# A two-layer block behind a Fourier transform: the first layer's split passes take 512 columns from two neighbouring chunks

## The chip, the cores and the metric

One Trainium2 chip; the program runs on one of its cores. The metric is the device time of one execution in microseconds (us); lower is better. Engines: PE (TensorE, matrix products), DVE (VectorE), ACT (ScalarE), POOL (GpSimd) and SP, which issues most DMAs.

## The reference

A batch of 8 sequences of 3008 rows and 256 columns goes through a two-dimensional Fourier transform, of which the real part is kept. Its 24,064 rows then go through two layers with a hard-swish between them:

```python
X = np.fft.fft(x, axis=1)
X = np.fft.fft(X, axis=2)
x = X.real.astype(np.float32).reshape(B * S, D)      # 24064 x 256
h = x @ w_in                                         # 256 -> 2048
g = h * np.clip(h + 3.0, 0.0, 6.0) / 6.0
return (g @ w_out).astype(np.float32)                # 2048 -> 256
```

## The kernel before

**Tiling.** The batch is taken as 4 pairs of sequences. A pair's transform along the rows has two stages (47 x 64 points): stage 1 multiplies folded inputs (POOL folds them) with a table and writes `z` to DRAM; stage 2 loads it back as `g`, multiplies it with a table `T`, and leaves `q`, 256 transformed rows at a time. The transform along the 256 columns is not done by itself: it is multiplied into `w_in` at the start (`W1`). Real input makes the result symmetric, so each `q` has an even and an odd part (block 0 and block 1), and one sum of products serves a row and its mirror image: even + odd and odd - even.

**Chunks and steps.** A pair has 12 chunks of 256 columns of `q` (the last: 194 for the first layer, 192 for the second). A chunk has 8 steps, each with two blocks of 128 of the 2048 features. So there are 4 x 12 x 8 = 384 steps. Steps 0 to 21 (`SPLIT` = 22) use plain f32 products for the first layer while the weights are prepared; from then on the first layer is split.

**The split first layer.** `split_q` and `split_w` (L612 to L617, L625 on) write `q` and `W1` as three parts each in a format that PE takes in one pass. A step's first layer is then 3 parts x 2 blocks x 2 feature blocks = 12 passes of 256 columns (`half_products`, L639): six even ones into the PSUM banks `u` and `v` (`even_half`), and, one step later, six odd ones into the same banks (`odd_half`). One row of the product is missing from the even part, the row part: `spread` broadcasts the row of `q` that it needs over all partitions by two DMAs (`qd`, `qn`), and `add_row` (L653) adds `qn` times the weights' column `WN` to `v` on DVE, 256 columns at a time, into `d`.

**Between the layers,** for the 512 columns (two feature blocks) of a step: ACT copies v to `y` (L669); DVE forms u + v (L670), ACT its relu (L708); DVE forms the other sign from the saved even part `s` (L679, L660), ACT its relu; then two gates on DVE (L711), min(t, 1) x h, write the activations `a`, the second one reversed for the mirrored rows.

**The second layer** is a Strassen-like scheme: POOL makes four sums `c` of the `a` (`combine`, L725), PE takes 7 products of f32 per step (`mlp2`, L758; each stands as two records) into 4 PSUM banks `acc` over the 8 steps. At a chunk's end ACT copies the banks to `e` (`copy_sums`, L775), POOL adds them up (`finish`, L725, L783), DVE transposes (L828) and SP stores.

**Order.** It is written out by hand, step by step. Step s runs the odd passes for step s + 2, the second layer of step s, the even passes for step s + 3 and `combine` for s + 1. The PSUM banks `a0`, `a1` (for u) and `y0`, `y1` (for v) alternate by step, and stage 1 (both banks of a turn) and stage 2 (one) borrow them. `beside` puts loads, spreads, stage 1 and stage 2 at fixed steps; `Feed` gives POOL the folding of the next pair where its estimated backlog allows it. Pools `ypool`, `gpool`, `qpool` and `zpool` have two buffers each, activations three (`apool`).

The order of a step's instructions, as far as it isn't plain from the above:

```python
odd_half(*chunk(s + 2))                  # PE odd passes; y, u + v, first relu
mlp2(*chunk(s), 0, 1)
stage1_parts(t); run(middle_fns, t)      # stage 1, stage 2
even_half(*chunk(s + 3), s + 3, ...)
add_row(*chunk(s + 3)); other_sign(*chunk(s + 2))
keep_even(*chunk(s + 3))
first_gate(*chunk(s + 2)); second_gate(*chunk(s + 2))
sums(); mlp2(*chunk(s), n, 7)            # combine, finish, store, split_q, folding; products
```

Of the kernel before, what the change touches and what calls it, by code (L numbers as in the profile page):

```python
# [49 lines left out]
WS = 2.0 ** 20  # L50
# [10 lines left out]
def kernel(  # L61
# [39 lines left out]
    ypool = ctx.enter_context(tc.tile_pool(name="ypool", bufs=2))  # L101
    zpool = ctx.enter_context(tc.tile_pool(name="zpool", bufs=2))
    gpool = ctx.enter_context(tc.tile_pool(name="gpool", bufs=2))
    tpool = ctx.enter_context(tc.tile_pool(name="tpool", bufs=1))
    qpool = ctx.enter_context(tc.tile_pool(name="qpool", bufs=2))
    spool = ctx.enter_context(tc.tile_pool(name="spool", bufs=2))
    apool = ctx.enter_context(tc.tile_pool(name="apool", bufs=3))
# [18 lines left out]

    ctx.enter_context(tc.manual_schedule())

    F1 = consts.tile([P, 5 * PB], F32, name="F1")
# [4 lines left out]
    W1 = consts.tile([P, 2, FF], F32, name="W1")  # L134
# [4 lines left out]
    class Pair:  # L139
        def __init__(self, p):  # L140
            self.p = p
            self.x, self.xr, self.y, self.z = {}, {}, {}, {}
            self.zd = {} if p == 0 else None
            self.zq = None
            self.g, self.q, self.qn = {}, {}, {}
# [6 lines left out]
    def x_tile(pool=xpool, tag="x"):  # L152
        return pool.tile([P, XC, D], F32, tag=tag, name="xt")
# [62 lines left out]
    def fold_half(hb, m, part, eng):  # L216
# [11 lines left out]
        y = ypool.tile([PX - 1, XC + 1, D], F32, tag="y", name="y")  # L228
# [46 lines left out]
    def bank(shape, name):  # L275
        if starting[0]:
            return ps_a.tile(shape, F32, tag="acc", name=name)
        if turn_of[0]:
            return ps_u.tile(shape, F32, tag=f"y{turn_of[0] % 2}", name=name)
        return lone_tile(shape, name)  # L280

    def other_bank(shape, name):
        if turn_of[0]:
            return ps_u.tile(shape, F32, tag=f"a{turn_of[0] % 2}", name=name)
# [4 lines left out]
    def stage1(pr, c):  # L289
# [17 lines left out]
        nc.scalar.copy(z[:, 0], ps[0][0:PB + PZ])  # L307
# [133 lines left out]
    def load_g(pr, gr):  # L441
        g = gpool.tile([P, 2 * KK, D + 1], F32, tag="g", name="g")
# [25 lines left out]

    def stage2_half(hb, gr, copy=nc.scalar.copy, ps=None, tab=None):

        vg, i = hb.b * NSG // 2 + gr // 2, gr % 2
        if i == 0:
            first.q[vg] = qpool.tile([P, 2, 2 * TB], F32, tag="q", name="q")
# [18 lines left out]
    def row_tile(pr, i):  # L492
        pr.qn[i] = qpool.tile([P, 2 * TB], F32, tag="qn", name="qn")

    def spread_half(hb, gr):
        vg, i = hb.b * NSG // 2 + gr // 2, gr % 2
        if i == 0:
            row_tile(first, vg)
        cs = slice(i * TB, (i + 1) * TB)
        qd = dpool.tile([1, 2 * TB], F32, tag="qd", name="qd")  # L500
        nc.sync.dma_start(out=qd[:, cs], in_=first.q[vg][P - 1:P, 1, cs])
        nc.sync.dma_start(out=first.qn[vg][:, cs], in_=qd[:, cs].to_broadcast([P, TB]))
        del hb.g[gr]

    def spread_by_pe(hb, ps, tab):
        row_tile(first, 0)
# [3 lines left out]
        nc.scalar.copy(first.qn[0][:, 0:TB], ps)  # L510
        del hb.g[0]

    def stage2(pr, gr, i, copy=nc.scalar.copy):

        if i == 0:
            pr.q[gr] = qpool.tile([P, 2, 2 * TB], F32, tag="q", name="q")
# [15 lines left out]
    def spread(pr, gr):  # L532
        row_tile(pr, gr)
        n = 2 * TB if gr < NG - 1 else 3 * P + 2 * NH
        qd = dpool.tile([1, 2 * TB], F32, tag="qd", name="qd")
        nc.sync.dma_start(out=qd[:, 0:n], in_=pr.q[gr][P - 1:P, 1, 0:n])
        nc.sync.dma_start(out=pr.qn[gr][:, 0:n], in_=qd[:, 0:n].to_broadcast([P, n]))
        del pr.g[gr]

    class Chunk:  # L540
# [3 lines left out]
        def __init__(self, pr, ck):  # L544
# [7 lines left out]
            self.a, self.c, self.acc, self.front, self.k = {}, {}, {}, {}, None  # L552
# [5 lines left out]
            self.blocks = [[(2 * b[j] + h, (k1[j], N1 - k1[j])[m]) for j in range(KC) for h in range(2)]  # L558
                           for m in range(2)]
# [7 lines left out]
    def mlp1_products(ch, fc, between=None):  # L567
# [3 lines left out]
        for blk, ps in ((0, u), (1, v)):  # L571
# [3 lines left out]
            for i in range(2):  # L575
                f = 2 * fc + i
                nc.tensor.matmul(ps[:, i, 0:nq], W1[r, blk, f * P:(f + 1) * P], q[r, blk, of:of + nq],  # L577
                                 start=True, stop=True)
        return u, v

    def activate(ch, fc, u, v, between=None):
        of, nq, qn = ch.ck % 2 * TB, ch.nq, ch.pr.qn[ch.ck // 2]
        s = spool.tile([P, 2, TB], F32, tag="s", name="s")
        for i in range(2):
            f = 2 * fc + i
            nc.vector.scalar_tensor_tensor(s[:, i, 0:nq], qn[:, of:of + nq], WN[:, f:f + 1], u[:, i, 0:nq],  # L586
# [3 lines left out]
        a = apool.tile([P, 2, 2, TB], F32, tag="a", name="a")  # L590
        t = spool.tile([P, 2, 2, TB], F32, tag="t", bufs=1, name="t")
        ch.a[fc] = a
# [11 lines left out]
    def split_q(ch):  # L604

        of, nq, q = ch.ck % 2 * TB, ch.nq, ch.pr.q[ch.ck // 2]
        ch.k = qpool.tile([P, 3, 2, TB], F32R, tag="k", bufs=2, name="k")
        high, low, rest = (ch.k[:, j, :, 0:nq] for j in range(3))
# [25 lines left out]
    def half_products(ch, fc, blk, u, v, order=(2, 0, 1)):  # L634
        nq = ch.nq
        for j in order:
            for i in range(2):
                fs = slice((2 * fc + i) * P, (2 * fc + i + 1) * P)
                nc.tensor.matmul((u, u, v)[j][:, i, 0:nq], KW[:, j, blk, fs], ch.k[:, j, blk, 0:nq],  # L639
                                 start=(blk == i == 0 and j != 1), stop=True, skip_group_check=True)  # L640

    def even_half(ch, fc, step, order):
        u = ps_u.tile([P, 2, TB], F32, tag=f"a{step % 2}", name="u")
        v = ps_u.tile([P, 2, TB], F32, tag=f"y{step % 2}", name="v")
        half_products(ch, fc, 0, u, v, order)
        ch.front[fc] = [u, v]

    def add_row(ch, fc):
        of, nq, qn, (u, v) = ch.ck % 2 * TB, ch.nq, ch.pr.qn[ch.ck // 2], ch.front[fc]
        d = spool.tile([P, 2, TB], F32, tag="d", bufs=1, name="d")  # L650
        for i in range(2):
            f = 2 * fc + i
# [892 lines left out]
```

## Time and profile before

| | before |
|---|---|
| median of 3 runs (lowest to highest) | 1831.02 us (1831.0 to 1833.35) |
| the profiled execution | 1830.63 us |
| its span in the profile | 1828.9 us |
| granted clock of PE, mean | 0.999 |
| busy share PE, DVE, POOL, ACT | 99%, 89%, 84%, 53% |
| busy PE weight loads | 89% |

A row of the timeline has the start in us, the duration in us, the engine, the line, the operation, the tiles as out<-in, the shape and how many were merged (x4); in brackets the idle time of the engine before it and what ended it. A merged row's duration runs from the first start to the last end, and PE's records overlap their neighbours: from start to start is what counts. A row of the groups has the count, the busy time in us, the mean ns of one, and the idle time before.

### The profile page before, as it was taken

The page shows a single profiled execution, that of the slowest core. Times are in us where ns is not written, and L with a number is a line of the kernel's source. Part 1 is how long each engine was busy: PE and PEld are TensorE (multiplying, and loading weights), DVE is VectorE, ACT ScalarE, POOL GpSimd, SP SyncE. Part 2 cuts the span into 40 slices and gives each one's busy share as a digit, 9 for nine tenths or more (in the row PEclk, how much of TensorE's full clock was granted, in tenths as well). Part 3 has the DMA queues.
Part 4 walks back from the last instruction along what each step waited for, and adds up shares of the span by engine and source line. Part 5 has one row for each costly group of instructions (what it writes and reads, how often), then busy time and mean ns, then how long its engine had stood idle before and what let it go on. Part 6 is the DMA issues. An engine that isn't in the chain of part 4 may idle for free.

```text
span 1828.9 us, 32501 instructions
## 1 busy us (share of the span) xinstructions
PE 1815.0 (99%) x10896; PEld 1619.8 (89%) x10896; DVE 1622.3 (89%) x3132; ACT 962.4 (53%) x1630; POOL 1529.7 (84%) x1694
## 2 busy tenths in 40 slices
PE   9999999999999999999999999999999999999998
PEld 6688888889998888899999888889999999999997
DVE  8978888888998888888998888888989989899898
ACT  6554555555555555554555555555555555555543
POOL 5687999998789999987778999998778778777885
PEclk9999999999999999999999999999999999999999
DMA  7433242321122313111122232310111111101001
GB/s 274 116 98 95 74 102 60 75 60 41 45 63 75 89 41 94 40 48 29 30 61 65 61 84 56 90 50 22 36 40 30 45 30 30 41 18 47 18 13 33
DMA packets 157629, 110.54 MB, mean 60 GB/s; under 512 B 121952, under 2 KB 136090, under 8 KB 157462
## 3 DMA queue, kind: packets, MB, share of 16 engines
q1 hardware_dynamic: 148710, 82.22, 18.0%
q0 software_dynamic: 7504, 25.65, 4.6%
q8 instruction: 87, 1.43, 0.3%
q10 hardware_dynamic: 1248, 0.59, 0.1%
q14 instruction: 80, 0.66, 0.1%
HBM read 71.93 MB, written 36.79 MB: 59 GB/s over the span
## 4 chain that ended last, share of the span: by engine, by line
PE 90%; DVE 5%; DMA 2%; issue 1%; ACT 1%; POOL 1%; SPq 0%; DVEq 0%; ACTq 0%; POOLq 0%
PE acc L758 58%; PE u L639 18%; PE v L639 9%; PE ps L526 2%; DVE a L711 1%; PE ps L296 1%; PE v L577 1%; DMA xt<-in_x_dram,IT 1%; PE u L577 1%; PE acc L735 1%; DVE d L653 1%; DVE s L660 0%; DVE s L586 0%; ACT t L708 0%; DVE u L593 0%
## 5 line engine op out<-in xcount | busy, mean ns | idle before, releaser
L758 PE MATMUL acc<-c,G 128*128 128x256 f32 (+1 forms) x3008 | 697.4, 375 | 0.0
L758 PEld LDWEIGHTS acc<-c,G 128*128 128x128 f32 x3008 | 559.9, 190 | 70.1 <-POOL c L725 2.4
L758 PE MATMUL acc<-a,G 128*128 128x256 f32 (+1 forms) x2256 | 599.8, 376 | 0.0
L725 POOL TENSOR_TENSOR c<-a 128x512 f32<-128x512 f32 (+1 forms) x375 | 471.7, 1258 | 129.9 <-DVE a L711 113.8
L639 PE MATMUL u<-k,KW 128*128 128x256 f32 (+1 forms) x2880 | 468.6, 285 | 0.9 <-DVE s L660 0.7
L708 ACT ACTIVATE t<-u,half 128x512 f32<-128x512 f32 (+1 forms) x384 | 260.6, 679 | 311.7 <-DVE u L670 255.9
L758 PEld LDWEIGHTS acc<-a,G 128*128 128x128 f32 x2256 | 373.0, 189 | 37.3 <-issue 17.5
L639 PE MATMUL v<-k,KW 128*128 128x256 f32 (+1 forms) x1440 | 403.0, 361 | 1.0 <-DVE a L711 1.0
L639 PEld LDWEIGHTS u<-k,KW 128*128 128x128 f32 x2880 | 393.5, 189 | 6.5 <-DVE s L660 1.4
L669 ACT COPY y<-v 128x512 f32<-128x512 f32 (+1 forms) x360 | 207.7, 577 | 319.8 <-PE v L639 319.8
L708 ACT ACTIVATE t<-v,half 128x512 f32<-128x512 f32 (+1 forms) x384 | 260.3, 678 | 201.1 <-DVE v L679 200.5
L670 DVE SCALAR_TENSOR_TENSOR u<-u,y 128x512 f32<-128x512 f32 (+1 forms) x360 | 247.1, 686 | 110.5 <-ACT y L669 96.5
L653 DVE SCALAR_TENSOR_TENSOR d<-qn,WN,v 128x256 f32<-128x256 f32 (+1 forms) x720 | 307.1, 468 | 9.9 <-PE v L639 9.6
L639 PEld LDWEIGHTS v<-k,KW 128*128 128x128 f32 x1440 | 265.1, 190 | 36.4 <-PE u L639 1.5
L725 POOL TENSOR_TENSOR c<-a,c 128x256 f32<-128x256 f32 (+1 forms) x375 | 269.5, 719 | 29.4
L725 POOL TENSOR_TENSOR c<-c,a 128x256 f32<-128x256 f32 (+1 forms) x375 | 269.2, 718 | 29.4
L679 DVE SCALAR_TENSOR_TENSOR v<-s,u 128x512 f32<-128x512 f32 (+1 forms) x360 | 246.4, 684 | 51.9 <-ACT t L708 51.3
L711 DVE SCALAR_TENSOR_TENSOR a<-t,u 128x512 f32<-128x512 f32 (+2 forms) x448 | 260.4, 593 | 3.2 <-ACT t L708 3.2
L711 DVE SCALAR_TENSOR_TENSOR a<-t,v 128x512 f32<-128x512 f32 (+1 forms) x480 | 263.1, 565 | 0.1
L660 DVE SCALAR_TENSOR_TENSOR s<-u,d 128x512 f32<-128x512 f32 (+1 forms) x360 | 242.6, 674 | 2.5
L725 POOL TENSOR_TENSOR e<-e 128x512 f32<-128x512 f32 (+2 forms) x184 | 182.8, 994 | 0.1
L775 ACT ACTIVATE e<-acc 128x512 f32<-128x512 f32 (+2 forms) x184 | 98.6, 538 | 4.7 <-PE acc L758 4.2
(140 smaller groups left out, 1090.4 us busy)
## 6 DMA issues: line engine op xcount, KB each, us to landing
out_dram<-o SPq DMA_DIRECT2D x744, 32.0 KB
T<-in_c_stage_dram SPq DMA_DIRECT2D x26, 512.0 KB
g<-zd SPq DMA_DIRECT2D x42, 256.0 KB
zd<-z SPq DMA_DIRECT2D x48, 192.0 KB
xt<-in_x_dram SPq DMA_DIRECT2D x21, 256.0 KB
qn<-qd SPq DMA_DIRECT2D x16, 256.0 KB
st<-in_moe_w_out_dram POOLq DMA_DIRECT2D x7, 512.0 KB, 5.2
xt<-in_x_dram SPq DMA_DIRECT2D x17, 192.0 KB
```

Source lines behind the costliest of these rows:

```text
L526: nc.tensor.matmul(ps[:, blk, u * P:n].rearrange("p (b k) -> p b k", b=2), g[:, kk, blk * (P + 1):blk * (P + 1) + P], T[gr][:, :, blk, kk, ...
L639: nc.tensor.matmul((u, u, v)[j][:, i, 0:nq], KW[:, j, blk, fs], ch.k[:, j, blk, 0:nq], start=(blk == i == 0 and j != 1), stop=True, skip_g ...
L653: nc.vector.scalar_tensor_tensor(d[:, i, 0:nq], qn[:, of:of + nq], WN[:, f:f + 1], v[:, i, 0:nq], op0=AL.mult, op1=AL.add)
L660: nc.vector.scalar_tensor_tensor(s[:, :, 0:nq], u[:, :, 0:nq], 1.0 + EPS, d[:, :, 0:nq], op0=AL.mult, op1=AL.add)
L669: nc.scalar.copy(yn, vn)
L670: nc.vector.scalar_tensor_tensor(un, un, 1.0 + EPS, yn, op0=AL.mult, op1=AL.add)
L679: nc.vector.scalar_tensor_tensor(vn, sn, -2.0, un, op0=AL.mult, op1=AL.add)
L708: nc.scalar.activation(t, h, AF.Relu, bias=half[:], scale=scale)
L711: nc.vector.scalar_tensor_tensor(dst, t, 1.0, h, op0=AL.min, op1=AL.mult)
L725: (eng or nc.gpsimd).tensor_tensor(out, in0, in1, op=AL.add)
L758: nc.tensor.matmul(ch.acc[i // 2][:, i % 2, 0:ch.n], G[:, i, fc, :], mv, start=(fc == 0 and i % 2 == 0), stop=(fc == NF - 1), skip_group_c ...
L775: nc.scalar.mul(e, acc, 1.0 / WS)
```

## The change

**Joint units.** A unit of the first layer is again 512 columns wide, but where it can it is one feature block of two neighbouring chunks in place of two feature blocks of one chunk. Its passes are then 6 of 512 columns in place of 12 of 256. Of the 360 units, 312 are joint and 48 alone (chunk 3 to 6 in part, and at the borders of pairs). A chunk's steps are joint with the chunk before and the chunk after by turns. `KQ`, a ring of three chunks, holds the split `q`, so that two chunks are one operand.

**Activations in a ring.** Half the activations of a chunk are made up to a chunk ahead, so they wait in `A`, 9 slots of 4 KB per partition. Room for it comes from single buffers in `ypool`, `gpool`, `qpool`, and from tiles of the first steps (`early`: `W1`, three `a`, one `q`, one `y`) that are given back at step 22. `place` says at which second-layer product each cycle begins: a cycle has one unit and mostly 7 products; the first five chunks and the first of each pair have nine cycles (seven with 6 products), each pair's last chunk seven of 8.

**Row part by ACT.** `seed` writes row x `WN` (from `QN`, a ring of four chunks) into the bank of v ahead of the even passes, which add to it, u first and v last. ACT then copies the even v (`copy_even`). `add_row` goes.

**Chunk ends.** `close` makes four of the final sums straight out of PSUM on DVE, beside two copies on ACT; POOL keeps two additions in place of five (`finish`).

**Other moves.** Stage 2's copy and one of stage 1's two copies go from ACT to DVE. The spread is made per chunk. Loads of `T` and `g` are put 7 and 6 steps ahead of a chunk's stage 2, that 7 steps ahead of its first unit. `Feed` reckons with other step times.

```diff
-    def add_row(ch, fc):
...
-            nc.vector.scalar_tensor_tensor(d[:, i, 0:nq], qn[:, of:of + nq], WN[:, f:f + 1], v[:, i, 0:nq],
-                                           op0=AL.mult, op1=AL.add)
+    class Unit:
+        def __init__(self, i, ch, fc, f=None, other=None):
...
+            if self.joint:
+                self.parts = sorted([(ch, f), (other, f)], key=lambda part: part[0].n_all % 3)
...
+    def passes(un, blk):
+        rows = P - blk
+        if not blk:
+            un.u = ps_u.tile([P, 2, TB], F32, tag=f"a{un.i % 2}", name="u")
+        for j in (2, 0, 1) if blk else (0, 1, 2):
+            o = (un.u, un.u, un.v)[j]
+            for i in range(1 if un.joint else 2):
+                nc.tensor.matmul(o[:] if un.joint else o[:, i, 0:un.nq], un.weights(j, blk, i, rows), un.moving(j, blk, rows),
+                                 start=blk == j == i == 0, stop=True, skip_group_check=True)
+    def seed(un):
+        un.v = ps_u.tile([P, 2, TB], F32, tag=f"y{un.i % 2}", name="v")
+        if un.joint:
+            f = 2 * un.fc + un.parts[0][1]
+            nc.scalar.activation(un.v[:], span(QN, [ch.n_all % 4 for ch, _ in un.parts]), AF.Identity, scale=WN[:, f:f + 1])
+            return
...
+    def copy_even(un):
+        nc.scalar.copy(un.d[:, :, 0:un.nq], un.v[:, :, 0:un.nq])
...
+    def close(ch, part):
...
+        if part == 0:
+            nc.scalar.mul(e[:, 0], acc(0), 1.0 / WS)
+        elif part == 1:
+            plus(e[:, 1], 1, e[:, 0])
+        elif part == 2:
+            nc.scalar.mul(e[:, 2:4], ch.acc[1][:, :, 0:ch.n], 1.0 / WS)
+        else:
+            plus(e[:, 5], 5, e[:, 0], -1.0)
+            plus(e[:, 4], 4, e[:, 5])
+            plus(e[:, 6], 6, e[:, 5])
...
-        nc.scalar.copy(z[:, 0], ps[0][0:PB + PZ])
+        nc.vector.tensor_copy(z[:, 0], ps[0][0:PB + PZ])
...
+            put(t, stage2, pr, gr, i, nc.vector.tensor_copy, at=middle_fns)
+            put(t + 1, spread, pr, gr, i)
...
-                feed.cycle(cost, (4.75 if s < SPLIT else 4.44) + 0.9 * (t in middle_fns) + 1.2 * (t in behind))
+        feed.cycle(cost, (4.75 if s < SPLIT else 4.33) + 0.9 * (s in middle_fns) + 2.05 * (s in behind))
...
+    while done < len(stream):
+        un, nx = (units[i] if i < len(units) else None for i in (cycle, cycle + 1))
...
+        ahead_of = min(size, 3 if parts or any(s in middle_fns for s in begun) or narrow else 2)
+        if un:
+            odd_half(un, (lambda: seed(nx)) if nx and not parts else None)
+        close_to(4)
...
+        for gen in parts:
+            next(gen)
+        for s in begun:
+            run(middle_fns, s)
+        products(ahead_of)
+        if nx:
+            if parts:
+                seed(nx)
+            passes(nx, 0)
+        products(size - ahead_of)
+        close_to(1)
+        if nx:
+            copy_even(nx)
+        if un:
+            other_sign(un)
+        if nx:
+            keep_even(nx)
+        close_to(3)
+        if un:
+            take_slots(un)
+            gates(un, 0)
+            gates(un, 1)
```

In `odd_half` the function `between` (the seed) stands behind the copy `y` in ACT's queue and ahead of the first relu.

More of the change, by code (lines that the diff above doesn't have):

```diff
@@ L515, in stage2 @@
         if i == 0:
[L516 removed]
+            q_tile(pr, gr)
         g = pr.g[gr]
@@ L632, in split_w @@
         return others
[L634 to L646, printed above, removed]
```

541 lines of the change are left out of this document (290 added, 251 removed).

## The prediction

> **What bounds the kernel now.** I read the page first (busy times, then the chain that ended last), then the timeline of one plain step of the steady part, engine by engine.
>
> ```profile
> span 1828.9 us, 32501 instructions
> ...
> PE 1815.0 (99%) x10896; PEld 1619.8 (89%) x10896; DVE 1622.3 (89%) x3132; ACT 962.4 (53%) x1630; POOL 1529.7 (84%) x1694
> ...
> PE 90%; DVE 5%; DMA 2%; issue 1%; ACT 1%; POOL 1%; SPq 0%; DVEq 0%; ACTq 0%; POOLq 0%
> ```
>
> PE is 99% busy and is 90% of the chain. Busy records overlap, so the question is how densely PE is fed. A step's PE records, with the first of the next step:
>
> ```profile
> 1007.18 0.59 PE L639 MATMUL v<-k,KW 128*128 128x256 f32 x2
> 1007.61 0.64 PE L639 MATMUL u<-k,KW 128*128 128x256 f32 x4
> 1008.08 0.59 PE L758 MATMUL acc<-a,G 128*128 128x256 f32 x2
> 1008.32 0.59 PE L639 MATMUL v<-k,KW 128*128 128x256 f32 x2
> 1008.75 0.64 PE L639 MATMUL u<-k,KW 128*128 128x256 f32 x4
> 1009.22 1.02 PE L758 MATMUL acc<-a,G 128*128 128x256 f32 x4
> 1010.08 1.89 PE L758 MATMUL acc<-c,G 128*128 128x256 f32 x8
> 1011.62 0.59 PE L639 MATMUL v<-k,KW 128*128 128x256 f32 x2
> ```
>
> The step lasts 1011.62 - 1007.18 = 4.44 us. It holds 12 passes of the split first layer (L639) and 7 second-layer products of two records each (L758). Start to start, four L758 records take 1010.08 - 1009.22 = 0.86, so 0.215 each; four L639 passes take 1009.22 - 1008.75 = 0.47, so 0.118 each. 14 x 0.215 + 12 x 0.118 = 3.01 + 1.42 = 4.43: nothing is left over, the step is PE's own work. The same step on VectorE and ScalarE:
>
> ```profile
> 1008.48 0.70 DVE L670 SCALAR_TENSOR_TENSOR u<-u,y 128x512 f32<-128x512 f32 x1
> 1009.09 0.86 DVE L653 SCALAR_TENSOR_TENSOR d<-qn,WN,v 128x256 f32<-128x256 f32 x2
> 1009.93 0.70 DVE L679 SCALAR_TENSOR_TENSOR v<-s,u 128x512 f32<-128x512 f32 x1
> 1010.54 0.68 DVE L660 SCALAR_TENSOR_TENSOR s<-u,d 128x512 f32<-128x512 f32 x1
> 1011.14 0.68 DVE L711 SCALAR_TENSOR_TENSOR a<-t,u 128x512 f32<-128x512 f32 x1
> 1011.73 0.68 DVE L711 SCALAR_TENSOR_TENSOR a<-t,v 128x512 f32<-128x512 f32 x1
> ```
>
> ```profile
> 1007.86 0.59 ACT L669 COPY y<-v 128x512 f32<-128x512 f32 x1 [0.95 <-PE v L639]
> 1009.21 0.69 ACT L708 ACTIVATE t<-u,half 128x512 f32<-128x512 f32 x1 [0.77 <-DVE u L670]
> 1010.66 0.69 ACT L708 ACTIVATE t<-v,half 128x512 f32<-128x512 f32 x1 [0.76 <-DVE v L679]
> ```
>
> VectorE runs nearly without a gap too: its rows here add up to 4.30 of the 4.44 us. So a faster PE would gain little with VectorE's queue as it is. ScalarE waits between its three rows (0.95, 0.77, 0.76).
>
> **The wide passes.** Counted in the two built programs, before has 3,936 passes of 256 columns and 384 of 194; after has 1,872 of 512, 456 of 256 and 120 of 194. That is 360 units of work in both: after, 312 are joint (six passes of 512) and 48 are alone (twelve narrow ones). The joint ones replace 290 units of 256 columns and 22 of 194. The row of the short ones, with its successor, and their sequel:
>
> ```profile
> 1795.33 0.61 PE L639 MATMUL u<-k,KW 128*128 128x194 f32 x4
> 1795.77 0.83 PE L758 MATMUL acc<-a,G 128*128 128x192 f32 x4
> 1796.44 1.46 PE L758 MATMUL acc<-c,G 128*128 128x192 f32 x8
> 1797.61 0.50 PE L639 MATMUL v<-k,KW 128*128 128x194 f32 x2
> ```
>
> Four passes of 194 columns take 0.44, so 0.110 each: 62 columns fewer save only 0.008, so a narrow pass is mostly a fixed cost. A 512-column pass is not in the trace. Its ends: 0.118 + 256 x 0.008/62 = 0.151 if that slope goes on, 0.236 if it costs two narrow ones. I take 0.216, the nearest record whose time does follow its columns, the second-layer one of 256 (0.215; at 192 columns, eight take 1.17 with the last hidden behind the next, 0.163 each). Then a joint unit costs 1.30 for 1.42: 290 x 0.120 + 22 x (12 x 0.110 - 1.296) = 34.8 + 0.5 = 35.3 us less. At 0.151 the bound moves to the loop below; at 0.236 nothing is gained.
>
> The Trainium skill (TensorE: Matmul & The Clock Gate, Back-to-back issue gap) gives a warm gap of N/2.4 + 2.5 ns: 216 ns for 512 columns, but 109 for 256. That speaks against the change: by it two narrow passes lose 2.6 ns to a wide one, and 1,872 passes are worth 4.9 us, not 35. The measured 0.118 decides; the same page says that in a stream of weight load and matmul both set the spacing.
>
> **ScalarE writes the row part ahead; VectorE's loop.** Two L653 of 256 columns go from VectorE (0.86 a unit). ScalarE gets a seed (row part into the PSUM bank of v, before the even passes add to it) and a copy of the even v. Nearest rows:
>
> ```profile
> L653 DVE SCALAR_TENSOR_TENSOR d<-qn,WN,v 128x256 f32<-128x256 f32 x656 | 283.5, 474 | 8.7 <-PE v L639 8.6
> ...
> L775 ACT ACTIVATE e<-acc 128x256 f32<-128x256 f32 x43 | 16.1, 376 | 0.0
> ...
> L626 ACT ACTIVATE high<-KW 128x512 f32<-128x512 f32 x8 | 4.8, 602 | 0.5
> ```
>
> L626 writes PSUM from SBUF in 0.60; a column operand costs up to 0.10 (L708's 0.69 against L669's 0.59). The seed is 0.60 to 0.70; I take 0.70. The skill's rule of thumb (ScalarE: Activation LUTs, Rules for kernel authors) is to keep multiplies and adds on VectorE; here 512 columns take ScalarE 0.6 to 0.7 and VectorE 0.86, so the trace disagrees, and the sum goes by the trace.
>
> Now the plain cycle after, t = 0 where the odd v pass starts. y starts 0.68 after a pair of passes that takes 0.43, so 0.47 after a wide one of 0.216: y 0.47-1.06. VectorE's u 1.09-1.79, first relu 1.82-2.51, v 2.54-3.24 (it waits for that relu; both read the bank of u), second relu 3.27-3.96. PE: odd passes to 0.65, two products to 1.51, even u to 1.94, even v to 2.16; its copy on ScalarE 2.42-3.01; VectorE's s from 3.15, gates from 3.75 and 4.34, the last ending at 5.02. PE needs 14 x 0.215 + 6 x 0.216 = 4.31. VectorE could start the next u at 4.93, a loop of 4.93 - 1.09 = 3.84. So PE still paces, 4.31 for 4.43, with 0.47 to spare. The seed follows y (0.97-1.67), needs the bank that the previous second gate leaves at 5.02 - 4.31 = 0.71, and is wanted at 1.94.
>
> Side work that VectorE gains: the four additions that close a chunk (0.47 each, as L653), a stage-2 copy (0.70, as L670), half the z copies. With the four transposes it had (taken as L653 too, at most) that is 1.9 + 0.7 + 1.9 = 4.5 a chunk, less about 0.09 for the overlap of neighbours (0.61 from start to start of two rows of 0.70) on nine, 3.6, or 0.45 a cycle: 3.84 + 0.45 = 4.29 if none of it fell into gaps. Most falls into the 0.75 between u and v. If the wide pass took 0.151, this 4.29 would hold the cycle where it is, so the low end changes nothing.
>
> **Where cover is short.** (1) A chunk's end. On ScalarE a copy of 256 columns (0.38, L775) now stands ahead of the copy of the even v, so s comes 0.19 later; one addition (0.38 from start to start) stands ahead of the gates. The second gate ends at 5.02 + 0.57 = 5.59, 1.28 into the next cycle, the next seed at 2.0, and even v waits 0.09. Then three additions fill the gap and the loop recovers. 33 chunks x 0.09 = 3. (2) Eight chunks (the first five and each pair's first) take nine cycles of six products: 12 x 0.215 + 12 x 0.118 = 4.0 with units alone. The even v ends at 2.71 for 2.16, its copy at 3.56, s runs from 3.59, the gates from 4.19 and 4.78, and the second ends at 5.46, 1.46 into the next cycle. No slack is left. A chunk's end adds 0.38: the bank is free at 1.84, two narrow seeds (0.38 and 0.10 each) end at 2.74, PE wants them at 2.47 (0.27); then the three additions put the end of s at 4.95, where the next odd u wants it at 4.51 (0.44). 0.7 x 8 = 6. Each pair's last chunk (16 x 0.163 + 1.30 = 3.9) I take at 0.8 x 3 = 2. (3) A step with stage 1 of the next pair:
>
> ```profile
> 1016.06 0.59 PE L639 MATMUL v<-k,KW 128*128 128x256 f32 x2
> ...
> 1017.48 1.09 PE L296 MATMUL ps<-y,F 47*64 47x512 f32 x8
> ...
> 1021.72 0.47 PE L639 MATMUL v<-k,KW 128*128 128x256 f32 x1
> ```
>
> It lasts 5.66, 1.22 over a plain one, all PE work. After, stage 1 borrows both banks that the last unit's gates must leave. In a plain cycle they are free at 0.71 against 0.65: 0.1. Behind a stage-2 cycle, which delays the even passes, at about 1.05: 0.4. Among six-product cycles at 1.46: up to 0.8. With 8, 8 and 8 of them (the last at a mean of 0.5) 0.8 + 3.2 + 4 = 8. The seed, behind the z copy on ScalarE, ends at about 3.7, PE wants it at 3.8. (4) The first chunks' ends now run through a serial chain of copy and additions: +2; the last seven steps have their units done ahead: -1.
>
> **At no cost.** POOL loses half of its end-of-chunk additions, and the step above holds no wait for it. Ring slots, g, T, q and y with one buffer: their loads are issued six or seven steps (26 us) before use, behind the reader of the last one. The spread is issued per chunk (47 pairs of DMAs for 27) a step after stage 2, six steps before the seed; a landing on the chain was
>
> ```profile
> 930.91 2.95 DMA qd<-q
> 933.92 2.67 DMA qn<-qd
> ```
>
> 5.6 us in all. Stage 2's own PE work is the same in both kernels (its eight records last from 966.77 to the next product at 967.66, 0.89):
>
> ```profile
> 966.77 1.05 PE L526 MATMUL ps<-T,g 128*128 128x128 f32 x8
> 967.66 1.03 PE L758 MATMUL acc<-a,G 128*128 128x256 f32 x4
> ```
>
> If the spread's cover went, the seed would hold ScalarE's queue: y, relus and closings behind it.
>
> **The sum.** The profiled execution took 1830.6 us (span 1828.9 and 1.7 around it), 0.4 under the median of 1831.0. 1830.6 - 35.3 + (3 + 6 + 2 + 8 + 2 - 1 = 20) = 1815.3, so 1815.
>
> **Rivals.** *All hidden* (0.17): the waits of (1) to (4) fit into gaps: 1795 to 1803. For it: 0.47 of slack per plain cycle. Against: the bank's release is fixed by the chain, not by load. *Eaten up* (0.09): the waits are nearly double, 1827 to 1835. *VectorE's loop takes over* (0.18): at each cycle u, relu, v, s and two gates follow each other; if PSUM traffic or handoffs add 0.07 to each of these five, the loop is 4.2, and 8 x 4.2 + 3.6 = 37.2 a chunk against before's 8 x 4.44 + 0.89 = 36.4: 45 x 0.8 = +36, 1867. It decides against the change from 8 x L + 3.6 = 36.4, L = 4.1. For it: VectorE was as full as PE. Against: 0.86 a unit leaves it, and its handoffs take 0.03 in the rows. *The wide pass saves nothing* (0.06): 0.236, hence 1830.6 + 20 = 1851. By the page's gap formula alone it would be 1830.6 - 4.9 + 20 = 1846, a part of this case.
>
> **Numbers.** Forecast 1815, chance 0.50, its own spread 1803 to 1827. 0.2% is 3.7 us, about what a measurement of this kernel tells from no change. Faster 0.50 + 0.17 = 0.67; same 0.09; slower 0.18 + 0.06 = 0.24. The range runs from all hidden, 1795, into the slower cases up to 1845, leaving out the worse half of the loop's case and the wide pass at full price.
>
> **What would show it.** Right: L639's successor with 512-column passes 0.216 apart, plain steps of 4.31 to 4.33, PE waiting on ScalarE's seed or VectorE's gate at chunk ends and stage 1. Wrong: passes 0.236 apart; plain steps paced by VectorE at 4.4 or more with PE gaps before even passes; PE waiting for POOL's c or for a DMA into g, T or QN.

## The result, and the profile after

| | median of the runs (us) | least to most | against before |
|---|---|---|---|
| before | 1831.2 | 1830.9 to 1834.2 | |
| after | 1840.3 | 1839.9 to 1842.1 | ratio 1.0047, 95% interval 1.0034 to 1.0060 |

The changed kernel is 0.5% slower, 9 us. The forecast was 1815, faster by 16. On the page of after, the span, the busy times and the chain that ended last:

```profile
span 1839.2 us, 28089 instructions
...
PE 1825.9 (99%) x9024; PEld 1534.6 (83%) x9024; DVE 1464.5 (80%) x2746; ACT 1320.1 (72%) x2238; POOL 1407.2 (77%) x1550
...
PE 94%; DVE 3%; ACT 1%; issue 0%; POOL 0%; another core or an unknown queue 0%; DVEq 0%; ACTq 0%; POOLq 0%
```

PE is 99% busy as before and carries more of the chain (94% for 90%), although it runs 1,872 instructions fewer. VectorE fell from 89% to 80%, ScalarE rose from 53% to 72%. So PE still sets the time; what matters is what its passes cost and where it waits. A plain cycle of PE in the timeline, from one odd v pass to the next:

```profile
1002.48 0.59 PE L676 MATMUL v<-KQ,KW 127*128 127x512 f32 x1
...
1002.91 0.62 PE L676 MATMUL u<-KQ,KW 127*128 127x512 f32 x2
...
1003.37 1.03 PE L807 MATMUL acc<-A,G 128*128 128x256 f32 x4
...
1004.05 0.81 PE L676 MATMUL u<-KQ,KW 128*128 128x512 f32 x2
...
1004.70 0.39 PE L676 MATMUL v<-KQ,KW 128*128 128x512 f32 x1
...
1004.93 0.59 PE L807 MATMUL acc<-A,G 128*128 128x256 f32 x2
...
1005.36 1.89 PE L807 MATMUL acc<-c,G 128*128 128x256 f32 x8
...
1006.90 0.59 PE L676 MATMUL v<-KQ,KW 127*128 127x512 f32 x1
```

It lasts 1006.90 - 1002.48 = 4.42 us, where before had 4.44 and the forecast 4.31. The even passes show the price: from the first u (1004.05) to the product behind the v pass (1004.93) is 0.88, of which the first 0.19 still belongs to the product in front (its second record starts just before the u pass); two u passes and one v pass share the rest, (0.88 - 0.19) / 3 = 0.23 each. The sharper figure comes from the 624 odd u passes: the median from their start to that of the next instruction is 0.232 (nine tenths of them lie under 0.234, whichever two slots of `KQ` they read), and so it is for the 312 even v passes (127 and 128 rows). Six of them are 1.39, twelve narrow ones were 1.42. With 14 x 0.215 that makes 4.40.

The edits on ScalarE cost what was forecast. Groups by line, mean of one in ns behind the busy time:

```profile
L690 ACT ACTIVATE v<-QN,WN 128x512 f32<-128x512 f32 x312 | 216.8, 695 | 16.0 <-DVE A L758 12.1 <-ACT y L710 0.3
...
L698 ACT COPY d<-v 128x512 f32<-128x512 f32 x360 | 209.7, 582 | 74.6 <-PE v L676 74.1
```

The seed takes 0.695 (0.70 forecast), the copy d 0.58 (0.59 forecast).

**Where the 10 us between the two spans are.** The 360 starts of VectorE's `u<-u,y` cut either trace into 359 cycles. A cycle's content is its PE work at these prices: a product 0.431 (0.325 in a last chunk), a pass 0.232 (512 columns), 0.1195 (256) or 0.112 (194), stage 2's eight records 0.89; what the cycle takes beyond its content is the excess. Stage 1 is left out of the content, so it stands in the excess whole.

| kind of cycle, after | count | mean length | excess in all |
|---|---|---|---|
| seven products | 228 | 4.42 | 3.2 |
| with stage 2 | 44 | 5.1 to 5.3 | 3.9 |
| six products | 45 | 4.07 | 3.5 |
| eight products (last chunk of the first three pairs) | 18 | 4.24 | 4.2 |
| with stage 1 | 24 | 5.96 | 38.7 |
| all | 359 | | 53.4 |

The same sum for before is 35.0, of which 24 cycles with stage 1, 1.22 over a plain one, make 29.3 and all others 5.7. So the waits between these starts grew by 53.4 - 35.0 = 18.4 us (38.7 - 29.3 = 9.4 at stage 1, 9.0 elsewhere). At the prices above the passes gave back 290 x (12 x 0.1195 - 6 x 0.232) - 22 x (6 x 0.232 - 12 x 0.112) = 12.2 - 1.1 = 11.1, not 35.3. That leaves 7.3 of the 1839.2 - 1828.9 = 10.3 by which the spans differ; the other 3.0 lie before the first of the starts and behind the last. A price that is 1 ns off on the 3,936 narrow passes of before would move 4 us between passes and waits, so the split is good to about that.

A cycle with stage 1 in the timeline of after, here a chunk's first cycle, and two rows of the waits of the whole trace (total, times, longest):

```profile
1045.02 0.63 PE L676 MATMUL u<-KQ,KW 127*128 127x512 f32 x2
1045.15 0.68 DVE L758 SCALAR_TENSOR_TENSOR A<-t,v 128x512 f32<-128x512 f32 x1
...
1045.58 1.39 PE L302 MATMUL ps<-y,F 47*64 47x512 f32 x8
...
1046.44 1.21 DVE L834 SCALAR_TENSOR_TENSOR e<-acc,e 128x256 f32<-128x256 f32 x3
...
1047.56 0.68 DVE L313 COPY z<-ps 112x512 f32<-112x512 f32 x1
...
1048.30 0.30 PEld L676 LDWEIGHTS u<-KQ,KW 128*128 128x128 f32 x2 [0.24 <-DVE z L313]
```

```profile
PEld v L676 <- ACT v L690: 11.1, 33, 0.5
...
PEld ps L302 <- DVE A L758: 6.9, 19, 0.4
```

The odd u passes end and stage 1 (L302) begins, but its second bank is held by the last gate of the unit before until 1045.15 + 0.68 = 1045.83, so that its eight records stretch over 1.39 where before's took 1.09. Then the even u pass waits for the z copy on VectorE (0.24), which stands behind three closing additions (1046.44). Such additions stand in only three of the 24 cycles. In the others the bank is the commonest wait: by the starts of the records, stage 1 is held up in 19 of 24, by 0.05 to 0.50, 4.7 us in all; in nine or so the even v pass then waits for the seed on ScalarE, by 0.07 to 0.23. (Idle times on PEld rows are those of the weight loads' queue. PE's own can be shorter: with stage 1 late, below, 0.65 there stands beside 0.24 on PE.)

### The profile page after: what moved, and what is told of

Its sections match the earlier page's. It is cut to its first block, busy times and chain, and to the rows that moved or that the text cites. A ratio compares the mean times of both kernels' runs of the same rounds, so it can differ in the third digit from the quotient of the medians.

```text
span 1839.2 us, 28089 instructions
## 1 busy us (share of the span) xinstructions
PE 1825.9 (99%) x9024; PEld 1534.6 (83%) x9024; DVE 1464.5 (80%) x2746; ACT 1320.1 (72%) x2238; POOL 1407.2 (77%) x1550
## 4 chain that ended last, share of the span: by engine, by line
PE 94%; DVE 3%; ACT 1%; issue 0%; POOL 0%; another core or an unknown queue 0%; DVEq 0%; ACTq 0%; POOLq 0%
PE acc L807 58%; PE u L676 18%; PE v L676 9%; PE ps L540 2%; PE ps L302 2%; PE acc L782 2%; PE v L590 1%; PE u L590 1%; DVE A L758 1%; DVE s L703 0%; PE spare L1012 0%; PE ps L368 0%; ACT v L690 0%; PE awake L1039 0%; PE ps L504 0%
## 5 line engine op out<-in xcount | busy, mean ns | idle before, releaser
L772 POOL TENSOR_TENSOR c<-A 128x512 f32<-128x512 f32 (+1 forms) x357 | 449.6, 1259 | 203.1 <-PE acc L807 163.8
L807 PE MATMUL acc<-A,G 128*128 128x256 f32 (+1 forms) x2160 | 559.5, 375 | 0.0
L676 PE MATMUL u<-KQ,KW 127*128 127x512 f32 (+4 forms) x1632 | 519.4, 409 | 0.4 <-DVE s L703 0.4
L807 PEld LDWEIGHTS acc<-A,G 128*128 128x128 f32 x2160 | 397.5, 189 | 78.6 <-issue 15.1
L676 PE MATMUL v<-KQ,KW 127*128 127x512 f32 (+4 forms) x816 | 356.7, 456 | 0.5
L676 PEld LDWEIGHTS u<-KQ,KW 128*128 128x128 f32 (+1 forms) x1632 | 289.5, 190 | 47.2 <-DVE s L703 3.7
L713 DVE SCALAR_TENSOR_TENSOR u<-u,y 128x512 f32<-128x512 f32 x360 | 250.2, 695 | 86.3 <-ACT y L710 78.9
L772 POOL TENSOR_TENSOR c<-c,A 128x256 f32<-128x256 f32 (+1 forms) x357 | 257.3, 721 | 28.0
L772 POOL TENSOR_TENSOR c<-A,c 128x256 f32<-128x256 f32 (+1 forms) x357 | 256.5, 719 | 28.0
L758 DVE SCALAR_TENSOR_TENSOR A<-t,v 128x512 f32<-128x512 f32 (+3 forms) x478 | 248.4, 540 | 0.0
L676 PEld LDWEIGHTS v<-KQ,KW 128*128 128x128 f32 (+1 forms) x816 | 150.4, 189 | 36.6 <-ACT v L690 11.1
```

The source lines that it names most:

```text
L676: nc.tensor.matmul(o[:] if un.joint else o[:, i, 0:un.nq], un.weights(j, blk, i, rows), un.moving(j, blk, rows), start=blk == j == i == 0, ...
L713: nc.vector.scalar_tensor_tensor(u, u, 1.0 + EPS, y, op0=AL.mult, op1=AL.add)
L758: nc.vector.scalar_tensor_tensor(dst, t, 1.0, h, op0=AL.min, op1=AL.mult)
L772: (eng or nc.gpsimd).tensor_tensor(out, in0, in1, op=AL.add)
L807: nc.tensor.matmul(ch.acc[i // 2][:, i % 2, 0:ch.n], G[:, i, fc, :], mv, start=(fc == 0 and i % 2 == 0), stop=(fc == NF - 1), skip_group_c ...
```

## The experiments

The theory after this reading (A): a split pass costs by its columns with a small fixed part, so that joining two saves a few ns, and the waits of the sum then show. The rivals: the pass is held to 0.232 by its surroundings (B) or by its weight load (C); and, for the waits, that the VectorE loop would have held the cycle anyway.

**Passes alone** (a kernel of its own: long rows of passes on PE, weights changing from pass to pass except in L50, no other work but a copy between rows).

> Passes alone on TensorE, nothing else of the kernel is computed: long rows of split-type (float32r) passes of 512, 480, 448, 384, 320, 256, 224, 192, 128 and 64 columns, then 512 and 256 with one weight block throughout, 512 with the banks alternating, 512 into 64 output rows, 512 from 64 input rows, bfloat16 passes of 512 and 256, float32 products of 512 and 256, 512-column passes alternating with float32 products of 256, and 512-column passes while ScalarE and VectorE read PSUM. Theory A (the pass itself costs by its columns): 512 columns 0.230 to 0.234 us start to start also here, 448 near 0.20, 384 near 0.175, 256 at 0.118, one straight line of some 0.45 ns a column from 256 up, and a floor near 0.11 below 256 that does not move with the weights being the same or not. Rival B (the surroundings in the kernel hold the pass back): 0.216 or less alone, and 0.23 only in the last two rows, where products alternate or other engines read PSUM. Rival C (a float32r pass carries a fixed cost of some 0.015 over a float32 record, from its weight load): 512 with one weight block, or into 64 rows, is 0.216, and the float32 product of 512 is 0.86 (four times 0.215).

Groups by line and shape:

```profile
L57 PE MATMUL b<-XR,WR 128*64 128x512 f32 x96 | 22.2, 392 | 0.0
L76 PE MATMUL b<-XR,WR 128*128 128x512 f32 x96 | 22.2, 391 | 0.0
L60 PE MATMUL b<-XR,WR 64*128 64x512 f32 x96 | 22.1, 387 | 0.0
L53 PE MATMUL b<-XR,WR 128*128 128x512 f32 x96 | 21.9, 389 | 0.0
L68 PE MATMUL b<-X,W 128*128 128x256 f32 x96 | 21.0, 380 | 0.7 <-ACT D L39 0.7
...
L43 PE MATMUL b<-XR,WR 128*128 128x448 f32 x96 | 19.6, 365 | 0.0
L43 PE MATMUL b<-XR,WR 128*128 128x384 f32 x96 | 16.8, 334 | 0.0
...
L43 PE MATMUL b<-XR,WR 128*128 128x320 f32 x96 | 14.4, 310 | 0.0
...
L50 PE MATMUL b<-XR,WR 128*128 128x256 f32 x96 | 11.7, 283 | 0.0
L43 PE MATMUL b<-XR,WR 128*128 128x224 f32 x96 | 11.0, 276 | 0.0
L43 PE MATMUL b<-XR,WR 128*128 128x192 f32 x96 | 11.0, 275 | 0.1
L43 PE MATMUL b<-XR,WR 128*128 128x128 f32 x96 | 10.9, 275 | 0.1
L64 PE MATMUL b<-XB,WB 128*128 128x256 bf16 x96 | 10.6, 272 | 0.7 <-ACT D L39 0.7
```

A row's busy time, less the overhang of its last record (0.16 us: a record of L53 lasts 0.389, the next starts after 0.227), through its count is the time from start to start. For the split type: 512 columns (L53) (21.9 - 0.16) / 96 = 0.227; 448, 0.202; 384, 0.173; 320, 0.148; 256 (L50) (11.7 - 0.16) / 96 = 0.120; and 224, 192 and 128 alike 0.112. From 256 up this is one line, (0.227 - 0.120) / 256 = 0.42 ns a column and 0.013 to 0.014 fixed; below it a floor that the columns do not move. Fewer output rows (L57) or input rows (L60) do not make a pass shorter, and one weight block throughout (L50, 256 columns: 0.120) hardly does (0.122 with changing blocks). While ScalarE and VectorE read PSUM (L76) it is 0.23. A float32 record of 256 takes 0.217 by the same reading, a bfloat16 pass of 256 0.109. Rows in which the granted clock was under 1.00 (64 columns, and the first passes of 512) are not used.

And between products, in the timeline:

```profile
362.49 0.58 PE L71 MATMUL b<-XR,WR 128*128 128x512 f32 x1
362.90 0.59 PE L72 MATMUL b<-X,W 128*128 128x256 f32 x2
363.15 0.58 PE L71 MATMUL b<-XR,WR 128*128 128x512 f32 x1
```

From one split pass to the next 363.15 - 362.49 = 0.66; two float32 records are 0.43 of it, so the pass is 0.23 beside products. Theory A holds: the pass itself takes 0.227 (a little under the 0.230 expected), not 0.216. Rival B has the smaller part: company adds 0.003 to 0.005, which over 1,872 passes is 6 to 9 us. Alone, a wide pass saves 2 x 0.120 - 0.227 = 0.013 against two narrow ones; in the kernel 0.007. Rival C is right that there is a fixed part, but a shorter weight load does not lower it: with 64 output rows (L57) the load's record is 134 ns instead of 188 and the pass takes 0.23. As each pass still has its load, where the fixed part comes from stays open.

The Trainium skill (TensorE: Matmul & The Clock Gate, Back-to-back issue gap) gives N/2.4 + 2.5 ns. The bfloat16 row (0.109 for 256 columns) agrees with it. The split type does not: 0.120 and 0.227 are some 0.011 above it.

**Two narrow passes for each wide one**

```diff
-            for i in range(1 if un.joint else 2):
-                nc.tensor.matmul(o[:] if un.joint else o[:, i, 0:un.nq], un.weights(j, blk, i, rows), un.moving(j, blk, rows),
+            for i in range(2):
+                w, mv = un.weights(j, blk, 0 if un.joint else i, rows), un.moving(j, blk, rows)
+                nc.tensor.matmul(o[:, i, 0:un.nq], w, mv[:, i] if un.joint else mv,
```

> The changed kernel with each wide pass made as two passes of 256 columns again, one for each chunk, with the same weights; units, order, waits and the other engines' work are as in the changed kernel. Theory A: a joint unit takes 12 x 0.118 = 1.42 us for 6 x 0.232 = 1.39, the plain cycle goes from 4.42 to 4.44 or 4.45, and the time from 1840 to 1844 to 1850. The prediction's price of 0.216 would make it 1840 + 312 x 0.120 = 1877. If the wide pass gave nothing at all, 1838 to 1842.

Measured 1852.8 (ratio to before 1.0115, 1.0098 to 1.0132): 12.5 over after, a little more than expected, a third of what 0.216 would make.

```profile
1500.59 0.59 PE L677 MATMUL v<-KQ,KW 127*128 127x256 f32 x2
...
1501.01 0.64 PE L677 MATMUL u<-KQ,KW 127*128 127x256 f32 x4
...
1502.83 0.40 PE L677 MATMUL v<-KQ,KW 128*128 128x256 f32 x2
...
1505.05 0.59 PE L677 MATMUL v<-KQ,KW 127*128 127x256 f32 x2
```

The plain cycle is 1505.05 - 1500.59 = 4.46. Where after has two u passes in a row, four stand here (1501.01); order and other work are the same. Less the products' 14 x 0.215 the cycle leaves 1.45 for twelve passes, where after's 4.42 leaves 1.41 for six: 0.04 in each of 312 units is the 12.5 us. So that is what joining is worth inside the new order. Against before it is 2.0 less, because 22 units that had passes of 194 columns (0.112) have passes of 256 here (22 x 12 x 0.0075): 10.5, near the 11.1 of the trace.

The same run prices the rest of the change by times alone. With narrow passes as before it is 1852.8 - 1831.4 = 21.4 slower than before, and 19.4 without those 2.0. The forecast had put 20 on this. Part of it is spread over all cycles: the same twelve passes and seven products took 4.44 in before's plain cycle and take 4.46 here.

**Five passes of six at half the columns**

```diff
+                m = TB if blk == j == 0 else 128
+                nc.tensor.matmul(o[:, :, 0:m] if un.joint else o[:, i, 0:un.nq], un.weights(j, blk, i, rows),
+                                 un.moving(j, blk, rows)[:, :, 0:m] if un.joint else un.moving(j, blk, rows),
```

> The changed kernel with five of a joint unit's six passes cut to the first 128 columns of each chunk (half of those products are left out); all else as in the changed kernel. It takes 5 x 0.114 = 0.57 us of PE's work out of each of 312 joint units, to see what holds the cycle once PE does not. By the prediction's loop on VectorE and ScalarE (3.84 a plain cycle, and 3.6 a chunk for side work) a plain cycle falls to 3.85 to 4.29 and the time to some 1750 to 1785. Rival (VectorE's loop is already 4.2 or more, and would have held the plain cycle even with passes of 0.216): plain cycles stay at 4.3 to 4.42, time 1815 to 1840.

Measured 1758.0 (ratio 0.9596, 0.9580 to 0.9612).

```profile
1640.41 0.47 PE L677 MATMUL v<-KQ,KW 127*128 127x256 f32 x1
...
1642.32 0.19 PEld L677 LDWEIGHTS v<-KQ,KW 128*128 128x128 f32 x1 [0.30 <-ACT v L692]
...
1644.51 0.47 PE L677 MATMUL v<-KQ,KW 127*128 127x256 f32 x1
```

The time is as expected. This cycle takes 1644.51 - 1640.41 = 4.10, and within it the even v pass waits 0.30 for the seed on ScalarE. A plain chunk (from one chunk's last transpose to the next's) takes 33.66 where after takes 36.25; the forecast's loop of 3.84 a cycle and 3.6 a chunk makes 34.3. The loop on VectorE and ScalarE was thus priced well, and a little high: it held nothing in the changed kernel.

**Passes at the price that was forecast** (as above with 238 columns of each chunk, 476 a pass)

> The changed kernel with five of a joint unit's six passes cut from 512 to 476 columns (the last 18 columns of each chunk are left out of those products); all else as in the changed kernel. 0.232 less 36 x 0.42 ns is 0.217 us, the price that the prediction had put on the wide pass. Theory A (only that price was wrong, the rest of the sum stands): the plain cycle falls from 4.42 to 4.34, 1560 passes save 0.015 each, 23 to 24 us, and the time is 1816 to 1818, near the forecast of 1815. Rival (the waits, too, are larger than the forecast's 20, hidden so far in a plain cycle that PE filled): 1822 to 1832.

Measured 1821.2 (ratio 0.9940, 0.9926 to 0.9953).

```profile
1501.27 0.57 PE L677 MATMUL v<-KQ,KW 127*128 127x476 f32 x1
...
1505.61 0.57 PE L677 MATMUL v<-KQ,KW 127*128 127x476 f32 x1
```

The plain cycle is 1505.61 - 1501.27 = 4.34, as expected, and a chunk 35.67. The time is between theory and rival: 19 of the expected 24 us came. The excess over content rose from 53.4 to 57.5 us, so 4 went into waits; and in the profiled execution, which is 2.3 above the median, the first unit comes 1.8 later. This kernel is 10 us faster than before, with one of a unit's six passes still at 512 columns. At 0.217 that one would take off up to 312 x 0.015 = 4.7 more, an estimate, and the time would be some 1816.5. So by this estimate the change, with the price as forecast, would have come out close to 1815.

**Stage 1 late** (behind two products; the even passes behind six; the gates ahead of the even sum)

```diff
+        if parts:
+            products(2)
         for gen in parts:
             next(gen)
...
-        products(ahead_of)
+        products(min(size - 2, 4) if parts else ahead_of)
```

> The changed kernel with stage 1 of the next pair moved behind the first two products of its cycle, the next unit's even passes behind the sixth, and the unit's gates ahead of the next unit's even sum in those 24 cycles. Theory (stage 1 waits for the two banks that the last unit's gates leave, the part (3) of the sum, 8 us): the cycles with stage 1 fall from 5.8 to 6.3 to 5.6 to 5.7, PE no longer waits ahead of them, and the time falls from 1840 to 1833 to 1836. Rival (the wait only moves on, to the even passes, whose seed stands behind the z copy, or to the next odd passes): 1838 to 1842.

Measured 1858.9 (ratio 1.0148, 1.0132 to 1.0163), worse by 19 us than after, outside both expectations. On the weight loads' queue:

```profile
1107.07 0.40 PE L676 MATMUL v<-KQ,KW 128*128 128x512 f32 x1
...
1108.14 0.19 PEld L676 LDWEIGHTS v<-KQ,KW 127*128 127x128 f32 x1 [0.65 <-ACT d L698]
...
1108.87 0.30 PEld L676 LDWEIGHTS u<-KQ,KW 127*128 127x128 f32 x2 [0.54 <-DVE s L703]
```

The bank is free in time (stage 1's records take 1.09 again), but now only two products stand between the last even pass (1107.07) and the next odd ones, which need the copy d and then the sum s: 0.65 and 0.54 of idle time on the weight loads' queue. Excess at stage 1: 54.4 for 38.7.

**All units alone**

```diff
-    joint[CHUNK1], joint[CHUNK1 + 1], joint[CHUNK1 + 2], joint[CHUNK1 + 3] = set(), {6}, {5}, {2, 4, 6}
-    for p in range(1, NP):
-        joint[p * NCK - 1], joint[p * NCK] = {5, 7}, {2, 4, 6}
+    joint = {}
...
-        sizes = [8] * 7 if n % NCK == NCK - 1 and n < NP * NCK - 1 else [6] * 7 + [7] * 2 if nine else [7] * 8
+        sizes = [7] * 8
```

> The changed kernel with no joint unit at all: each unit takes both blocks of one chunk, twelve passes of 256 columns, so the cycles of six products and of eight go too, and every cycle has seven. Ring, seeds on ScalarE (two of 256 columns a unit), copies and closings stay. Against the run with two narrow passes (1852.8) it takes away the cycles with six products, priced at 6 and 2 us in the sum, and part of stage 1's wait, and adds 0.26 to ScalarE for the second seed. Theory (the waits sit where the sum put them): plain cycles of 4.44 to 4.46, 1840 to 1846. Rival (the waits are in every cycle, from the seeds and copies on ScalarE): 1850 to 1856, plain cycles above 4.46.

Measured 1854.8 (ratio 1.0124, 1.0109 to 1.0140): the rival's time, but not for its reason. Plain cycles are 4.45; the cycles with stage 1 are the long ones, this one among the longest:

```profile
1000.61 0.60 PE L676 MATMUL v<-KQ,KW 127*128 127x256 f32 x2
...
1001.65 1.59 PE L302 MATMUL ps<-y,F 47*64 47x512 f32 x8
...
1006.87 0.59 PE L676 MATMUL v<-KQ,KW 127*128 127x256 f32 x2
```

1006.87 - 1000.61 = 6.26, and stage 1's records stretch over 1.59, where before's took 1.09: they wait for their banks in between (in most of the 24 they take 1.31). Over all, 24 such cycles have an excess of 42.9, against 29.3 before. There are no cycles of six products here, so their part in stage 1's wait, which the sum had priced highest, is not what makes it. In the pairs' last chunks, where this run has cycles of seven products and after cycles of eight, the excess is 14.7 us for 4.2 in after, which speaks for the cycles of eight.

**Stage 1 in the middle** (two products, stage 1, two products, even passes, the rest; s between the gates)

```diff
+        if parts:
+            products(2)
         for gen in parts:
             next(gen)
...
+        if parts:
+            products(2)
+            ahead_of = 4
...
```

> The changed kernel with stage 1 of the next pair behind the first two products of its cycle, two more products behind it, then the next unit's even passes, then the rest of the products; in these 24 cycles the even sum s stands between the two gates on VectorE. In the run with stage 1 late, the next odd passes waited 0.65 for the copy d and 0.54 for the sum s, because only two products stood between them and the even passes. Theory (both waits fit: two products, 0.86, cover the bank that stage 1 needs, two more the z copies and the seed, three, 1.29, the copy and the sum): a cycle with stage 1 takes 1.16 to 1.3 over a plain one instead of 1.6, 24 x 0.3 to 0.45 is 7 to 10 us, and the time is 1830 to 1834, about that of the kernel before. Rival (the chain of copy, seed, copy and sum is longer than a cycle's products whatever the order): 1838 to 1850.

Measured 1843.9 (ratio 1.0068, 1.0054 to 1.0082): the rival.

```profile
1050.01 0.69 DVE L313 COPY z<-ps 112x512 f32<-112x512 f32 x1
...
1050.67 0.69 ACT L690 ACTIVATE v<-QN,WN 128x512 f32<-128x512 f32 x1
...
1051.41 0.19 PEld L676 LDWEIGHTS v<-KQ,KW 128*128 128x128 f32 x1 [0.36 <-ACT v L690]
...
1053.31 0.30 PEld L676 LDWEIGHTS u<-KQ,KW 127*128 127x128 f32 x2 [0.29 <-DVE s L703]
```

The bank is free in time here too. But the even v pass waits 0.36 for the seed (1050.67), which waits for the z copy (1050.01), and the next odd u pass 0.29 for s (both on the weight loads' queue). The excess at stage 1 is 42.4, for 38.7 in after and 54.4 with stage 1 late: in neither order did the wait shrink, it only moved. That the chain from stage 1 over z copy, seed, v pass, copy and sum to the next odd passes is too long for any order fits this, but two orders do not show it.

**No seed beside stage 1** (in these cycles VectorE adds the row part to v after the even pass, as before the change; stage 1 behind one product, the closing additions behind the z copies)

```diff
-                                 start=blk == j == i == 0, stop=True, skip_group_check=True)
+                                 start=blk == i == 0 and (j == 0 or j == 2 and not un.seeded), stop=True,
+                                 skip_group_check=True)
...
+            nc.vector.scalar_tensor_tensor(un.d[:], span(QN, [ch.n_all % 4 for ch, _ in un.parts]), WN[:, f:f + 1],
+                                           un.v[:], op0=AL.mult, op1=AL.add)
```

> The changed kernel with, in the 24 cycles with stage 1 alone, the seed undone: the even v pass starts its bank, and VectorE adds the row part afterwards (one operation of 512 columns for a joint unit), as in the kernel before; stage 1 stands behind one product, the even passes behind two more, the closing additions behind the z copies, and the even sum between the two gates. The other cycles are untouched. In the runs so far the even v pass waited for z copy and then seed, one behind the other. Theory (that chain is what holds the stage 1 cycles in every order tried): without the seed they take 5.6 to 5.7 for 5.8 to 6.3, 24 x 0.25 to 0.4 is 6 to 9 us, and the time is 1831 to 1835. Rival (the banks' release by the gates, or the sum s for the next odd passes, holds them as well): 1838 to 1844.

Measured 1839.1 (ratio 1.0038, 1.0025 to 1.0052), the rival's time. Thirteen of the 24 cycles fall to 5.64 or less, as the theory has it; but the three in the first cycle of a chunk rise to 6.6 to 6.7:

```profile
1046.44 1.20 DVE L848 SCALAR_TENSOR_TENSOR e<-acc,e 128x256 f32<-128x256 f32 x3
...
1048.75 0.74 DVE L706 SCALAR_TENSOR_TENSOR d<-QN,WN,v 128x512 f32<-128x512 f32 x1
...
1049.55 0.19 PEld L676 LDWEIGHTS v<-KQ,KW 127*128 127x128 f32 x1 [0.68 <-DVE d L706]
```

The three closing additions (1.20) now push the unit's gates back, d comes late, and the odd v pass waits for it. So the time moved by 1 us only. As the order changed along with the seed, what the seed alone is worth is not shown.

**And not in a chunk's first cycle** (the same, with one condition more)

```diff
-            if pieces and pieces[0][0] <= s and s not in middle_fns and s not in behind:
+            if pieces and pieces[0][0] <= s and s not in middle_fns and s not in behind and steps[s][2]:
```

> As the run before (no seed in the cycles with stage 1), and stage 1 of a next pair is put off by one cycle where it would fall on the first cycle of a chunk. There VectorE still has the three closing additions, 1.2 us, in front of the unit's sums, and the run before showed 6.0 to 6.7 for these cycles against 5.63 for the others. Theory (the remaining wait of stage 1 is these additions): the cycles at 6.0 and above go, but for the two of the first pair's second half that stand at fixed places, and the time falls from 1839 to 1834 to 1837. Rival (the additions hold the next odd passes anyway, or the later stage 1 meets stage 2): 1838 to 1841. The kernel before, at 1831.5, is reached in neither.

Measured 1836.7 (ratio 1.0029, 1.0018 to 1.0040), at the upper end of the theory's range. The excess at stage 1 falls to 32.9, 3.6 above before's 29.3. This is the best version with wide passes that was run; the kernel before stays ahead by 5 us.

## Why the prediction was wrong, point by point

- **What bounds the kernel**: right. PE's own work held the plain cycle, before and after, and with passes of half the columns the cycle falls to 4.10, where PE begins to wait for the seed.
- **The price of the wide pass is the step that failed.** Of the ends 0.151 and 0.236 the prediction took 0.216, from the float32 record of 256 columns. The pass takes 0.232 in the kernel, 0.227 alone; the term of -35.3 came out at -10.5 (by the run with two narrow passes) or -11.1 (by the prices of the trace). The mistake was in "a narrow pass is mostly a fixed cost". It came from two rows, 256 and 194 columns, 0.008 apart. But 194 lies on the floor of 0.11, where columns no longer count; a slope through a point on a floor is no slope. Above the floor the fixed part is 0.014 of 0.120, so that nearly all of a narrow pass is columns, and joining two saves at most one fixed part (in the kernel, half of it). The float32 record was near in time but of another type. The row of the split type itself, taken twice, gave the high end, and that was the right neighbour.
- **The formula that spoke against it.** The prediction set the gap formula of the Trainium skill (TensorE: Matmul & The Clock Gate, Back-to-back issue gap) aside because it misses the narrow pass (109 ns for 118). By it a wide pass saves 2.5 ns (the prediction wrote 2.6), some 5 us in all. The traces show that it misses the wide pass too, by 11 ns alone and 16 in the kernel, and two narrow ones by 20 or so. So its 5 us was too low, but much nearer to the measured 11 than the forecast's 35.3 was.
- **Seed and copies**: right, 0.695 and 0.58 for 0.70 and 0.59. But together they take ScalarE 1.28 a unit, where VectorE did the row part in 0.86 in two operations, and in 0.74 in one of 512 columns (the runs without the seed). The loop: 34.3 a chunk forecast, at most 33.66 shown.
- **Short cover**: 20 forecast; 18.4 between the cycles and 3.0 outside them by the trace, 19.4 by the run with narrow passes. The size was right, the parts less so. Stage 1: 8 forecast, 9.4 measured. Its reason, the bank's release, holds in 19 of 24 cycles, for 4.7 of this; the seed and in three cycles the z copy come behind it, also without cycles of six products. Those cycles: 6 forecast, 5.4 measured (3.5, and 1.9 in those with stage 2). A pair's last chunks: 2 forecast, but the excess of 5.0 there is no growth, as nearly all of before's 5.7 lies in its own last chunks. The others (chunk ends and first chunks, 4 net) measured 4.4.
- **At no cost**: the spread and single buffers show no wait of PE in after. POOL's c holds the weight loads' queue for 3.2 us in all, for 2.4 before.
- **The rivals**: "the wide pass saves nothing", at 0.06 and 1851, is what happened, in a milder form. It deserved far more. "VectorE's loop takes over" is refuted by the kernel with half the columns. That 1840 lies within the stated 1795 to 1845 is luck: the range reached so high for the case of VectorE's loop, and left out the wide pass at full price.

The sum with one number exchanged, 1830.6 - 11 + 20 = 1839.6, lies 0.7 us below the measured 1840.3.

## What to carry to other kernels

A price that is not in the trace is bounded by the same instruction type first, even if the other type's row is nearer in time. Two rows give a slope only if neither lies on a floor: look for a third, or take "the same work in fewer instructions costs the same" as the likeliest case. And an edit that pays for its gain with waits should be priced at the gain's low end: here some 20 us of waits were well founded in the trace, and the 35 us against them hung on one choice between 0.151 and 0.236.

## What the runs showed of the hardware

- A split-type pass takes some 0.014 us and 0.42 ns a column alone from 256 to 512 columns, and 0.11 alike at 224, 192 and 128: 256 is about the least at which columns count. 64 rows in or out, or one weight block throughout, make no pass clearly shorter.
- In the kernel the wide pass takes 0.232 for 0.227 alone (0.23 beside float32 products), while a narrow one takes 0.119 to 0.120 in both. Why the wide one differs stays open.
- Work that borrows an accumulator bank between two units puts its copies into the chain that leads from bank to bank. In five orders (two of them without the seed there) the 24 cycles with stage 1 exceeded their other work by 32.9 to 54.4 us, against 29.3 before, while PE's own work in them was the same.
